# Moving a weight matrix to the end of the load stream: where the product of w2 is loaded and summed

## The chip, the cores and the metric

One core of one Trainium2 chip. The metric is the device time of one execution in microseconds. PE is the matmul engine and PSUM the memory that it adds its results up in; DMA is the loading from memory. The profile records for PE a granted clock, a share of full speed: 1.0 is called warm here, 0.5 cold. In the first measurement the kernel before took 194.74 to 194.83 us in four runs. Later batches ran on other chips, each beside its own runs of the kernel before (medians 194.63, 194.84, 195.00 for a single run, and 194.69), so experiments are compared with the kernel before of their own batch. Its single runs scattered more in those batches than in the first: from 194.44 to 195.08 over eleven runs, from 194.56 to 195.22 over eleven, from 194.60 to 195.05 over eight.

## The reference, cut to what matters

Attention for one new token in two batch rows, over the last 4096 positions of 8 key/value heads, plus a dense layer on the same normalised input, plus the input:

```python
def reference(A_x, A_k_cache, A_v_cache, A_wq, A_wo, B_x, B_w1, B_b1, B_w2):
    xn = _layernorm(A_x, axis=-1)                    # 2 rows of 448
    return A_x + attention(xn, k_cache, v_cache, wq) @ wo + mish(xn @ w1 + b1) @ w2
# w2: 1792 x 448, bf16. Keys and values used: 16 (head, row) pairs, 2 MB of keys and 2 MB of values each.
```

Nearly all of it is loading: 77.7 MB for 3810 instructions of work. Everything is summed in two PSUM banks, `psA[0]` and `psA[1]`, of 2 x 224 values each: the input, the w2 product and the wo product.

## The kernel before

The parts that matter (cuts marked with `...`):

```python
def add(n, lhsT, rhs, **flags):                 # every psA matmul: 2 weight columns, 224 moving
    nc.tensor.matmul(psA[n][:, :], lhsT=lhsT, rhs=rhs, skip_group_check=True, **flags)

def load_dense():                               # near the start: w1, then w2 whole
    dense["w1"] = ...
    dense["w2"] = v_tile(NX * NF * D)...
    nc.sync.dma_start(out=dense["w2"], in_=B_w2.rearrange("(x q c) d -> q x c d", x=NX, q=P))

def dense_out():                                # 28 psA matmuls, at step 1 of 18
    for x in range(NX):
        for c in range(NF):
            for n in range(NO):
                add(n, act_bf[:, c, x, :], w2_sb[:, x, c, n * DO : (n + 1) * DO], ...)

def values(i):                                  # 64 matmuls: 128 weight columns, 2 moving
    ...
def mix(kvh):                                   # 8 psA matmuls with wo rows
    ...

for i in range(NK + KA):                        # NK = 16 heads x rows, KA = 2
    if i + 2 < NK: load_k(i + 2)
    if i < NK:
        load_v(i, parts=1 if i < NK - 1 else 2)         # the last values in two transfers
        if b == Bsz - 1:
            load_wo(kvh, parts=1 if i < NK - 1 else 2)
        ...                                             # scores of head i
    if i == 1: dense_out()
    if i >= KA:
        values(i - KA)
        if b == Bsz - 1: mix(kvh)
# then copy psA[0], psA[1] to SBUF and store
```

All large loads are issued in this order by one engine, SyncE, and in the traces here PE's matmuls follow one another in the order of the program. So at the end PE has, in a fixed line: values of the last head, then its wo product.

The softmax here doesn't subtract the row's maximum and nothing guards it: scores larger than these inputs give would overflow.

## Time and profile before

| what | value | from |
|---|---|---|
| median time | 194.76 us | four runs |
| span of the profiled execution | 192.7 us | the page |
| share of DMA in the chain that ended last | 96% | the page |
| last landing of values | 187.21 us | the chain in order of time |
| PE done | 190.19 us | the chain in order of time |
| w2 product, in the middle | 28 matmuls in 2.84 us | PE's timeline |

The lines themselves, and how these times follow from one another, stand in the prediction.

### The profile page before, as it was taken

What the parts mean: (1) busy time and instruction counts of PE and PEld (TensorE: products, weight loads), DVE (VectorE), ACT (ScalarE), POOL (GpSimd) and SP (SyncE); (2) the same over time, 40 slices, a digit from 0 to 9 for tenths busy, and PEclk for the clock granted to TensorE, in tenths of its full rate; (3) what the DMA queues carried; (4) which work ended last, traced back from release to release, by engine and by line L of the source; (5) the groups of instructions that cost most, each with busy time, mean ns of one, the idle gap of its engine ahead of it and who ended that gap; (6) DMA issues with size and microseconds to landing.
All of it is one profiled execution on the core that took longest, in us unless ns stands there. A gap on an engine that the chain in (4) does not pass through costs nothing.

```text
span 192.7 us, 3810 instructions
## 1 busy us (share of the span) xinstructions
PE 130.4 (68%) x1624; PEld 81.3 (42%) x1624; DVE 102.2 (53%) x137; ACT 25.5 (13%) x69; POOL 24.8 (13%) x138
## 2 busy tenths in 40 slices
PE   0242993999827985499709881797449592898854
PEld 0142381466513654246504651364324452364752
DVE  4605506996638390929264753838091744748101
ACT  5000110112200211012200220021101110021100
POOL 7004320022110112002200210020200200000000
PEclk9999996699995799669975998599957979589965
DMA  6999999999999999999999999999999999999960
GB/s 211 424 447 408 427 427 435 428 435 402 431 422 428 425 415 428 435 418 414 429 425 432 420 416 430 428 425 411 428 432 428 403 434 422 432 414 429 410 253 2
DMA packets 7674, 77.90 MB, mean 404 GB/s; under 512 B 741, under 2 KB 2793, under 8 KB 3050
## 3 DMA queue, kind: packets, MB, share of 16 engines
q1 hardware_dynamic: 7652, 77.66, 96.1%
q8 instruction: 12, 0.20, 0.4%
q14 instruction: 4, 0.03, 0.0%
q10 hardware_dynamic: 6, 0.01, 0.0%
HBM read 77.67 MB, written 0.00 MB: 403 GB/s over the span
## 4 chain that ended last, share of the span: by engine, by line
DMA 96%; PE 1%; SPq 1%; issue 0%; ACT 0%; DVE 0%
DMA v<-in_A_v_cache_dram 51%; DMA k<-in_A_k_cache_dram 18%; DMA wo<-in_A_wo_dram 17%; DMA v<-in_B_w_dram 10%; PE psA L201 1%; PE o L411 1%; SPq L109 0%; SPq L325 0%; ACT res L484 0%; DVE oT L422 0%; SPq L336 0%
## 5 line engine op out<-in xcount | busy, mean ns | idle before, releaser
L352 DVE STREAM_TRANSPOSE kt<-k 128x2048 f32<-128x2048 f32 x32 | 73.5, 2300 | 48.9 <-DMA k<-in_A_k_cache_dram 48.9
L364 PE MATMUL sc<-kt,qdiag 128*128 128x512 bf16 x256 | 75.0, 443 | 14.4 <-DVE kt L352 14.3
L364 PEld LDWEIGHTS <-qdiag 128*128 128x128 bf16 x256 | 26.1, 111 | 50.5 <-issue 24.1
L374 ACT ACTIVATE p<-sc 128x512 bf16<-128x512 f32 x32 | 19.1, 597 | 144.8 <-PE sc L364 140.9
L244 POOL COPY qdiag<-qrep 32x8 bf16<-32x8 bf16 x128 | 21.0, 186 | 125.3 <-PE sc L364 109.8
L201 PE MATMUL psA<-wo,oT 128*2 128x224 bf16 x64 | 12.5, 370 | 31.3 <-DVE oT L422 31.3
L411 PEld LDWEIGHTS <-v 128*128 128x128 bf16 x1024 | 27.9, 97 | 6.3 <-DMA v<-in_A_v_cache_dram 3.0
L411 PE MATMUL o<-pT,v 128*128 128x2 bf16 x1024 | 28.1, 163 | 2.7 <-DMA v<-in_A_v_cache_dram 2.7
L385 DVE STREAM_TRANSPOSE pT<-p 128x512 bf16<-128x512 bf16 x32 | 21.4, 671 | 0.0
L201 PEld LDWEIGHTS <-oT 128*2 128x2 bf16 x64 | 6.5, 111 | 34.6 <-DVE oT L422 32.0
L393 PEld LDWEIGHTS den<-hsel,rs 128*128 128x128 f32 x64 | 11.7, 227 | 3.8 <-issue 2.1
L401 DVE RECIPROCAL rec<-den 128x2 f32<-128x2 f32 x16 | 2.5, 153 | 18.7 <-PE den L393 18.7
L393 PE MATMUL den<-hsel,rs 128*128 128x2 f32 x64 | 9.4, 252 | 0.0
L215 PE MATMUL qT_ps<-xs,v 128*128 128x4 bf16 x112 | 3.3, 166 | 6.1 <-DMA v<-in_A_wq_dram 6.1
L422 DVE TENSOR_TENSOR oT<-o,rec 128x4 bf16<-128x4 f32 x16 | 2.1, 134 | 8.5 <-PE o L411 8.5
L374 ACT ACTIVATION_READ_ACCUMULATOR p<-sc 128x1 f32 x32 | 6.2, 194 | 0.0
L215 PEld LDWEIGHTS <-v 128*128 128x128 bf16 x112 | 3.1, 104 | 6.6 <-DMA v<-in_A_wq_dram 6.6
L224 DVE CAST qT<-qT_ps 128x64 bf16<-128x64 f32 x1 | 0.2, 225 | 7.0 <-PE qT_ps L215 7.0
L169 PE MATMUL xnT_ps<-ident,xn_bf 2*128 2x2 bf16 x7 | 0.5, 166 | 5.0 <-DVE xn_bf L133 5.0
L270 PE MATMUL hT_ps<-xs,v 128*128 128x4 bf16 x49 | 3.7, 195 | 0.0
L270 PEld LDWEIGHTS <-v 128*128 128x128 bf16 x49 | 3.2, 149 | 0.3
L201 PE MATMUL psA<-v,act_bf 128*2 128x224 bf16 x28 | 2.8, 259 | 0.0
(40 smaller groups left out, 22.5 us busy)
## 6 DMA issues: line engine op xcount, KB each, us to landing
k<-in_A_k_cache_dram SPq DMA_DIRECT2D x16, 2048.0 KB, 32.5
v<-in_A_v_cache_dram SPq DMA_DIRECT2D x15, 2048.0 KB, 34.8
v<-in_B_w_dram SPq DMA_DIRECT2D x2, 1568.0 KB, 21.2
wo<-in_A_wo_dram SPq DMA_DIRECT2D x7, 448.0 KB, 31.8
v<-in_A_wq_dram SPq DMA_DIRECT2D x1, 2048.0 KB, 7.8
v<-in_A_v_cache_dram SPq DMA_DIRECT2D x2, 1024.0 KB, 29.9
v<-in_A_wq_dram SPq DMA_DIRECT2D x1, 1536.0 KB, 11.1
wo<-in_A_wo_dram SPq DMA_DIRECT2D x2, 224.0 KB, 24.1
```

The source lines that it names most:

```text
L201: nc.tensor.matmul(psA[n][:, :], lhsT=lhsT, rhs=rhs, skip_group_check=True, **flags)
L215: nc.tensor.matmul(qT_ps[:, hh, e, :], lhsT=wq_v[s][:, hh, e, :], rhs=xs[:, s, :, :].rearrange("p x b -> p (x b)"), start=(s == 0), stop=( ...
L244: nc.gpsimd.tensor_copy(out=tv[rows, :, e, j * Q : j * Q + rep], in_=qrep[rows, :, h0 : h0 + rep, e, x, b],)
L270: nc.tensor.matmul(hT_ps[:, c, :, :].rearrange("p x b -> p (x b)"), lhsT=w1_v[:, s, c, :], rhs=xs[:, s, :, :].rearrange("p x b -> p (x b)" ...
L352: nc.vector.transpose(out=kt[:].bitcast(FP32), in_=k[:, half * TH * Dh : (half + 1) * TH * Dh].bitcast(FP32),)
L364: nc.tensor.matmul(psc[:], lhsT=qdiag[i % NW][:, n * NE + e, :], rhs=ktv[:, n, e, :, :], start=(n == 0 and e == 0), stop=(n == NB - 1 and ...
L374: nc.scalar.activation(out=p_sb[:], in_=psc[:].rearrange("p t c -> p (t c)"), func=ACT.Exp, scale=scale, accum_out=state["rs", i][:, s % N ...
L385: nc.vector.transpose(out=pT[:], in_=p_t.pop(s)[:])
L393: nc.tensor.matmul(den[:], lhsT=rs[:, n : n + 1].to_broadcast([P, P]), rhs=hsel[:], start=(n == 0), stop=(n == NH - 1),)
L401: nc.vector.reciprocal(out=state["rec", i][:], in_=den[:])
L411: nc.tensor.matmul(po[:, c, :], lhsT=vv[:, t, c, :], rhs=pTv[:, th, 0:rep], start=(t == 0 and c == 0), stop=(t == T - 1), skip_group_check ...
L422: nc.vector.tensor_tensor(out=oT[:, :, :, b], in0=po[:], in1=state.pop(("rec", i))[:].unsqueeze(1).to_broadcast([P, ND, rep]), op=ALU.mult,)
```

## The change

The intent: after the last bytes land there should be as little work as possible. So w2, which needs nothing but the dense activations that have long been ready, is loaded last, in three parts (14, 10 and 4 matmuls' worth, into a buffer that held keys before), and its product closes the sum. Only the third part (4 matmuls) is then behind the last landing. In exchange the last values and the last wo rows are each one transfer again.

```diff
-        dense["w2"] = v_tile(NX * NF * D).rearrange(...)
-        nc.sync.dma_start(out=dense["w2"], in_=B_w2.rearrange(...))
+    W2 = ((0, 0, NF), (1, 0, NF - 2), (1, NF - 2, NF))
+    def load_w2():
+        t = k_pool.tile([P, T * Dh], BF16, tag="k", name="k")
+        ...
+        for x, lo, hi in W2:
+            nc.sync.dma_start(out=t[:, x, lo:hi, :], in_=w2_in[:, x, lo:hi, :])
...
-            load_v(i, parts=1 if i < NK - 1 else 2)
+            load_v(i)
...
-                load_wo(kvh, parts=1 if i < NK - 1 else 2)
+                load_wo(kvh)
+            if i == NK - 1:
+                load_w2()
...
-        if i == 1:
-            dense_out()
         if i >= KA:
             values(i - KA)
             ...
+    dense_out()
```

`dense_out` now runs by part, bank and chunk, and its last matmul on each bank closes the group.

More of the change, by code (lines that the diff above doesn't have):

```diff
@@ L251, with load_w1 @@
     dense = {}
-    def load_dense():
+    def load_w1():
         dense["w1"] = v_tile(NS * HF).rearrange("p (s n) -> p s n", s=NS)
@@ L258, in load_dense @@
         )
-        dense["w2"] = v_tile(NX * NF * D).rearrange("p (x c d) -> p x c d", x=NX, c=NF)
-        nc.sync.dma_start(
-            out=dense["w2"], in_=B_w2.rearrange("(x q c) d -> q x c d", x=NX, q=P)
-        )
+    W2 = ((0, 0, NF), (1, 0, NF - 2), (1, NF - 2, NF))
+    def load_w2():
+        t = k_pool.tile([P, T * Dh], BF16, tag="k", name="k")
+        t = t[:, 0 : NX * NF * D].rearrange("p (x c d) -> p x c d", x=NX, c=NF)
+        w2_in = B_w2.rearrange("(x q c) d -> q x c d", x=NX, q=P)
+        for x, lo, hi in W2:
+            nc.sync.dma_start(out=t[:, x, lo:hi, :], in_=w2_in[:, x, lo:hi, :])
+        dense["w2"] = t
     def dense_in():
@@ L305, in dense_out @@
         w2_sb = dense.pop("w2")
-        for x in range(NX):
-            for c in range(NF):
-                for n in range(NO):
+        for x, lo, hi in W2:
+            for n in range(NO):
+                for c in range(lo, hi):
                     add(
@@ L313, in dense_out @@
                         start=False,
-                        stop=False,
+                        stop=(x == NX - 1 and c == NF - 1),
                     )
@@ L328, in load_k, with load_v, load_wo @@
         k_t[i] = t
-    def load_v(i, parts=1):
+    def load_v(i):
         kvh, b = heads[i]
-        t = v_tile(T * Dh).rearrange("p (t d) -> p t d", t=T)
-        vin = A_v_cache[b, kvh, s0:Sk, :].rearrange("(p t) d -> p t d", p=P)
-        for u in range(parts):
-            ts = slice(u * T // parts, (u + 1) * T // parts)
-            nc.sync.dma_start(out=t[:, ts, :], in_=vin[:, ts, :])
-        v_t[i] = t
-    def load_wo(kvh, parts=1):
+        t = v_tile(T * Dh)
+        nc.sync.dma_start(
+            out=t, in_=A_v_cache[b, kvh, s0:Sk, :].rearrange("(p t) d -> p (t d)", p=P)
+        )
+        v_t[i] = t.rearrange("p (t d) -> p t d", t=T)
+    def load_wo(kvh):
         w = wo_pool.tile([P, rep, ND * D], BF16, tag="wo", name="wo")
@@ L342, in load_wo @@
         win = A_wo[r0 : r0 + rep * Dh, :].rearrange("(h p c) d -> p h (c d)", h=rep, p=P)
-        for u in range(parts):
-            hs = slice(u * rep // parts, (u + 1) * rep // parts)
-            nc.sync.dma_start(out=w[:, hs, :], in_=win[:, hs, :])
+        nc.sync.dma_start(out=w[:], in_=win)
         wo_t[kvh] = w
@@ L439, in mix @@
                         start=False,
-                        stop=(kvh == Hkv - 1 and h == rep - 1 and c == ND - 1),
+                        stop=False,
                     )
@@ L446 @@
     load_k(0)
-    load_dense()
+    load_w1()
     load_k(1)
```

## The prediction

> **What bounds the kernel now.** I read the page first (busy shares, the slices, the chain that ended last), then the chain in order of time, then PE's timeline and the windows of the last 13 us.
>
> ```profile
> PE   0242993999827985499709881797449592898854
> PEclk9999996699995799669975998599957979589965
> DMA  6999999999999999999999999999999999999960
> GB/s 211 424 447 408 427 427 435 428 435 402 431 422 428 425 415 428 435 418 414 429 425 432 420 416 430 428 425 411 428 432 428 403 434 422 432 414 429 410 253 2
> DMA 96%; PE 1%; SPq 1%; issue 0%; ACT 0%; DVE 0%
> ```
>
> From the second slice to slice 38 the DMA engines are 90% busy or more and move 402 to 447 GB/s; 96% of the final chain is DMA. The kernel is one stream of 77.7 MB. PE, 68% busy, has room in the middle. So the time is: start, the stream, and what is left to do after the last bytes. The end of the chain in order of time:
>
> ```profile
> 156.59 30.62 DMA v<-in_A_v_cache_dram
> 187.21 0.05 issue
> 187.26 1.02 PE o L411 x32
> 188.28 0.02 issue
> 188.31 0.18 DVE oT L422
> 188.48 0.04 issue
> 188.53 1.67 PE psA L201 x8
> 190.19 0.02 issue
> 190.22 0.34 ACT res L484
> ```
>
> The second half of the last values lands at 187.21; 32 value matmuls, the normalisation and 8 wo matmuls follow, PE is done at 190.19: a tail of 2.98 us. The last 2.5 us (190.2 to 192.7) are the copy and the output's way home, the same in both kernels. The second wo half is issued at 166.38 and takes 21.9 us (the smallest time to landing of wo), so the stream itself ends at 188.3, in the shadow of the value matmuls.
>
> PE's timeline and the windows at the end:
>
> ```profile
> 180.32 0.93 PE L201 MATMUL psA<-wo,oT 128*2 128x224 bf16 x8 [0.26 <-DVE oT L422]
> ...
> 182.29 1.75 PE L411 MATMUL o<-pT,v 128*128 128x2 bf16 x64 [0.50 <-DMA v<-in_A_v_cache_dram]
> 184.78 1.01 PE L411 MATMUL o<-pT,v 128*128 128x2 bf16 x32 [0.73 <-DMA v<-in_A_v_cache_dram]
> 187.26 1.01 PE L411 MATMUL o<-pT,v 128*128 128x2 bf16 x32 [1.47 <-DMA v<-in_A_v_cache_dram]
> 188.53 1.65 PE L201 MATMUL psA<-wo,oT 128*2 128x224 bf16 x8 [0.26 <-DVE oT L422]
> ```
>
> ```profile
> 182.00:184.00 2.00, 1.71 (x64) 1.67 (x64) 0.00 (x0) 0.00 (x0) 0.00 (x0) 1.00 1.01 422
> 184.00:186.00 2.00, 1.06 (x34) 0.93 (x32) 0.17 (x1) 0.00 (x0) 0.00 (x0) 0.53 0.85 331
> 186.00:188.00 2.00, 0.74 (x28) 0.75 (x29) 0.00 (x0) 0.00 (x0) 0.00 (x0) 0.50 0.25 91
> 188.00:190.20 2.20, 1.92 (x19) 1.02 (x15) 0.52 (x2) 0.00 (x0) 0.00 (x0) 0.50 0.00 0
> ```
>
> In these rows the columns after PE, PEld, DVE, ACT, POOL are the granted clock, the DMA share and GB/s. The same eight 224-column matmuls take 0.93 us at clock 1.0 and 1.65 us at clock 0.5. The clock fell at about 184.1 though PE had just run 64 value matmuls[...]. DMA falls from 0.85 to 0.25 before the last landing[...].
>
> [...] cold at 184.1, and elsewhere the full clock came back at 64.6, 5.4 us after dense work had begun at 59.22. [...] (1.65 and 0.93 us less one latency of 0.39 and 0.26, over 7: 180 and 96 ns; 180 includes a shorter first step). [...]
>
> **The change part by part.** w2 is 1792 x 448 x 2 B = 1.606 MB. The rate at the end, from the last two value halves, is 1.049 MB in 187.26 - 184.78 = 2.48 us, 423 GB/s.
>
> *Bytes.* None is added or removed. All traffic before the last wo rows now lands earlier by 1.606 MB / 423 GB/s = 3.80 us, w2 comes after, the stream ends again at about 188.3.
>
> *Landings, counted back from 188.3.* The third part of w2 (229 KB) at 188.3, the second (573 KB) at 187.8, the first (803 KB) at 186.4, wo at 184.5, the last values, now whole, at 187.21 - 3.80 = 183.4.
>
> *Removed.* The 28 w2 matmuls in the middle (2.84 us at clock 1.0, 39.15 to 41.99) leave a stretch in which PE is not the bound: no gain. Gone from the end: the wait for the second value half and the tail after it.
>
> *Added at the end on PE, in program order.* 64 value matmuls begin at 183.4 + 0.05 and take 1.75 us (27 ns each at either clock: 32 took 1.01 cold, 64 took 1.75 warm): 185.2. Normalisation and start of the next burst, as from 188.28 to 188.53, 0.25: 185.45. Then 8 wo matmuls and 28 for w2 on the same two banks, 36 in a row. Cold, 36 x 0.187 + 0.2 for the last one's latency = 6.9 us: 192.4. Warm, 36 x 0.096 + 0.2 = 3.7: 189.1.
>
> *Which clock.* Everything before is earlier by 3.8, so the last score burst (before: done at 178.3) is done at 174.5; then come 128 value matmuls, 8 for wo, and an idle stretch from about 180.2 to 183.4. That is less work than what lost the clock before, so the burst starts cold. [...] Back at 188.0: 14 done, 22 x 0.096 + 0.2 = 2.3, end 190.3. Back at 191.4: 32 done, end 192.0. Mean about 191.1. [...] it ends at 192.4; I give that 30%.
>
> *Sum.* 0.7 x 191.1 + 0.3 x 192.4 = 191.5, against 190.19 before: +1.3 us. The last w2 landing (188.3 plus 4 matmuls, 0.8 us: 189.1) is **not** the last wait in this account: w2's first part is there at 186.4, while PE gets to it at 185.45 + 8 x 0.187 = 186.9. The change turns a tail bound by a landing into one bound by a cold PE.
>
> **The rivals.**
>
> *1. The intended gain.* PE keeps up, and only four matmuls follow the last landing: 189.1, 1.1 us less than before, 193.7. For it: after the last bytes there is much less to do than 72 matmuls' worth of waiting in two halves. Against: 36 matmuls in 188.3 - 185.45 = 2.9 us need 80 ns each, under even the warm 96. At full clock the two limits meet; it needs a warm PE at 185.4. About 10%.
>
> *2. The stream itself changes.* Without w2 early, a value buffer is free sooner, and transfers might be issued sooner. But the stream is never short of work: the transfers wait 30 us from issue to landing and DMA is 90% busy throughout, so hidden: 0. A stall because w2 waits for a key buffer: the keys of head 12 were turned long before, also 0. [...]
>
> *3. Landing of the last values later than 183.4*[...]. Every 0.1 us there is 0.1 us at the end, as PE is in line behind it.
>
> **Range and chances.** Rounding the sum down a little for the chance of rival 1: 194.77 + 1.15 = 195.9. The low end, 194.4, is warm soon with a stream slightly faster; the high end, 197.3, is a burst cold throughout (+2.2) with a little more. 2% is 3.9 us, more than any of these: within 2% 0.96, faster 0.01, slower 0.03.
>
> **What would show it right or wrong.** The last values land at about 183.4 and the 64 value matmuls start there without a second wait. The last 36 psA matmuls run without a gap of any DMA from about 185.4, with granted clock 0.5 at first and 187 ns apart, and PE ends 1 us or so later than 190.19. The final chain should then hold about 6 us of PE in place of 2.7, and its last DMA should be the values, not w2. Times of single runs should scatter more than the 0.09 us of before[...]. It is wrong if the last wait of PE is for w2 (rival 1: the clock then is 1.0 in the burst), if the last values land much from 183.4, or if the stream ends elsewhere than at 188.3.

The sum: 0.7 x 191.1 + 0.3 x 192.4 = 191.5 against 190.19, so +1.3 us, rounded down to 1.15. Its terms: the clock should come back between 188.0 and 191.4 (of which 191.1 is the mean end), and a burst cold to the end (192.4) should have 30%. Read both as guesses, and "less work than what lost the clock before" as an estimate from one fall, that at 184.11 in the kernel before. The spacings in it are measured in the kernel before: in the burst from 188.53, at clock 0.5, matmuls start 187 ns apart; at 180.32, at clock 1.0, eight of them take 0.93 us, less one of 0.26 and over 7, 96 ns.

## The result, and the profile after

The changed kernel took 194.94, 195.39, 195.69 and 195.82 us: median 195.54, against 194.76. The ratio is 1.0035, 95% interval 1.0011 to 1.0060. (A ratio here is the mean time of one kernel's fast runs over that of the other's of the same rounds, so not quite the ratio of the medians.) So it is slower by about 0.7 us, well within 2%; and its runs scatter over 0.88 us where those of the kernel before scatter over 0.09 in this batch (over 0.45 to 0.66 in the later ones).

The page's rate of transfer and its chain, for the kernel after:

```profile
GB/s 221 426 440 416 439 434 424 421 424 414 431 424 434 417 421 424 434 415 420 431 428 428 421 416 424 428 417 428 424 428 406 445 424 424 416 425 424 399 215 2
DMA 94%; PE 4%; SPq 0%; issue 0%; ACT 0%; DVE 0%
```

The stream is what it was: no slice of the middle falls under 406 GB/s (402 before). In the chain DMA's share went from 96 to 94%, PE's from 1 to 4%. The end of the chain in order of time (start, length, what):

```profile
151.81 31.74 DMA v<-in_A_v_cache_dram
183.55 0.05 issue
183.60 1.88 PE o L414 x64
185.48 0.02 issue
185.50 0.17 DVE oT L425
185.68 0.04 issue
185.72 4.92 PE psA L201 x36
190.64 0.02 issue
190.66 0.33 ACT res L488
```

The last DMA in the chain is the values, not w2. From 183.60 on PE works 6.8 us with no wait but the normalisation. The windows of the same stretch (after PE, PEld, DVE, ACT and POOL: granted clock, DMA share, GB/s):

```profile
182.00:184.00 2.00, 0.40 (x15) 0.41 (x16) 0.00 (x0) 0.00 (x0) 0.00 (x0) 0.50 1.03 404
184.00:186.00 2.00, 1.74 (x58) 1.59 (x55) 0.16 (x1) 0.00 (x0) 0.00 (x0) 0.50 0.76 305
186.00:188.00 2.00, 2.00 (x13) 1.34 (x11) 0.00 (x0) 0.00 (x0) 0.00 (x0) 0.50 0.28 111
188.00:190.00 2.00, 2.00 (x21) 1.66 (x20) 0.00 (x0) 0.00 (x0) 0.00 (x0) 0.90 0.00 0
```

From 186 to 188 PE is fully busy and gets through 13 matmuls at clock 0.5; from 188 to 190, at 0.90 on average, through 21. DMA has nothing left to move after 188: the last of the three w2 transfers is issued at 167.6 and takes 20.8 us, so it is there at about 188.4, 2.2 us before PE is done. PE is behind the data, at half clock.

### The profile page after: what moved, and what is told of

Its sections match the earlier page's. It is cut to its first block, busy times and chain, and to the rows that moved or that the text cites. A ratio compares the mean times of both kernels' runs of the same rounds, so it can differ in the third digit from the quotient of the medians.

```text
span 193.2 us, 3810 instructions
## 1 busy us (share of the span) xinstructions
PE 134.6 (70%) x1624; PEld 83.4 (43%) x1624; DVE 102.3 (53%) x137; ACT 25.4 (13%) x69; POOL 24.8 (13%) x138
## 4 chain that ended last, share of the span: by engine, by line
DMA 94%; PE 4%; SPq 0%; issue 0%; ACT 0%; DVE 0%
DMA v<-in_A_v_cache_dram 35%; DMA k<-in_A_k_cache_dram 35%; DMA wo<-in_A_wo_dram 18%; DMA v<-in_A_wq_dram 5%; PE psA L201 3%; PE o L414 1%; SPq L109 0%; ACT res L488 0%; DVE oT L425 0%; SPq L339 0%; SPq L331 0%
## 5 line engine op out<-in xcount | busy, mean ns | idle before, releaser
L367 PE MATMUL sc<-kt,qdiag 128*128 128x512 bf16 x256 | 78.4, 459 | 12.7 <-DVE kt L355 12.0
L367 PEld LDWEIGHTS <-qdiag 128*128 128x128 bf16 x256 | 27.2, 115 | 50.8 <-issue 28.7
L396 PEld LDWEIGHTS den<-hsel,rs 128*128 128x128 f32 x64 | 13.1, 255 | 4.3 <-issue 2.5
L396 PE MATMUL den<-hsel,rs 128*128 128x2 f32 x64 | 10.6, 270 | 0.0
L201 PE MATMUL psA<-k,act_bf 128*2 128x224 bf16 x28 | 3.5, 290 | 0.0
## 6 DMA issues: line engine op xcount, KB each, us to landing
k<-in_B_w_dram SPq DMA_DIRECT2D x1, 560.0 KB, 25.2
```

Of the source, the lines that this page charges most:

```text
L367: nc.tensor.matmul(psc[:], lhsT=qdiag[i % NW][:, n * NE + e, :], rhs=ktv[:, n, e, :, :], start=(n == 0 and e == 0), stop=(n == NB - 1 and ...
L396: nc.tensor.matmul(den[:], lhsT=rs[:, n : n + 1].to_broadcast([P, P]), rhs=hsel[:], start=(n == 0), stop=(n == NH - 1),)
```

## The experiments

The theory, called A in the expectations: PE's line of work after the last values sets the end, and its clock sets how long that line is. Its rival, B: the landing of w2 sets the end. All outputs are right.

The trace keeps a record of PE's granted clock: it is 1.0 or 0.5. Near the end it rises at 170.46 and falls at 184.11 in the profile of the kernel before; in the changed kernel's it rises at 174.76, falls at 181.59 and rises again at 188.41. For the experiments it is read from its mean over stretches of 1 or 2 us. What sets the times of these switches is not shown here.

### The changed kernel again (after_again, after_third)

No edit.

> The changed kernel itself, once more, as the yardstick of this chip. Theory A (the end is set by PE's line of 64 value and 36 psA matmuls at a halved clock, and by when the clock comes back): median 195.3 to 195.8, single runs scattered over 0.5 us or more, granted clock 0.5 at the start of the 36. Theory B (the end is set by the landing of w2's third part): the same median, but scatter like that of the kernel before, 0.1 us, and a DMA as the last wait of PE.

> One more look at the changed kernel[...]. Theory A: the burst of 36 begins at clock 0.5 again; the later in it the clock comes back (0.5 to 1.0), the later the end, by about half of the delay.

Measured: median 195.29, runs from 194.96 to 196.57, ratio to the kernel before 1.0043 (1.0021 to 1.0064). The single look took 195.17. The median of the first was a hair under the range expected of it, the scatter is there, and in both profiles the burst starts cold, at 185.66 and 185.79. The full clock comes back at about 188.3 in the first profile (mean clock 0.50 from 186 to 188, 0.92 from 188 to 190), at about 188.8 in the second (0.50, then 0.80); PE is done at 190.56 and 190.87. The later return goes with the later end. The profiles did not catch the slowest run (196.57), so what that one did is not seen. Its span on the core is 194.1 us, against 193.1 to 193.8 of the other five: so about half a microsecond of its excess lies outside the span, and PE's work lies within it.

### A warm PE (e1_warm) and the same instructions without columns (e2_narrow)

The kernel holds eight PSUM tiles, one of which is free after the start. Fillers are written there:

```diff
+    def keep_busy(n, cols):
+        for _ in range(n):
+            nc.tensor.matmul(state["spare"][:, 0:cols], lhsT=ident[:, :],
+                rhs=qdiag[0][:].rearrange("p n c -> p (n c)")[:, 0:cols],
+                start=True, stop=True, skip_group_check=True)
...
+        if i == NK:
+            state["spare"] = ps_m.tile([P, 512], FP32, tag="m", name="spare")
+            keep_busy(4, 512)          # e2_narrow: 2 columns in place of 512
+        if i == NK + 1:
+            keep_busy(9, 512)          # e2_narrow: 2 columns in place of 512
         if i >= KA:
             values(i - KA)
```

> The changed kernel with 13 matmuls of 512 columns into a bank that nobody reads, 4 ahead of the values of the last head but one and 9 ahead of the last values, where PE waits for a DMA anyway. Theory A: the clock is 1.0 when the 36 psA matmuls begin, they run 96 ns apart, PE ends near 189.3 instead of 190.6 to 191.5, so 193.6 to 194.0, less than the kernel before; and the scatter shrinks to 0.1 or 0.2 us. Theory B: no gain, 195.5.

> As e1_warm, with the same 13 matmuls of 2 columns each: the instructions without the streamed columns. Theory A: they do not hold the clock, so as the changed kernel, 195.3 to 195.8, with its scatter. If instead the mere presence of instructions on PE (or a changed issue) made e1_warm faster, this one is faster too, near 194.

Measured: e1_warm took 193.73, 194.04, 194.81, 195.28, 195.33 and 195.52, ratio 1.0008 (0.9982 to 1.0035). The expected speed was reached by two runs of six, and the scatter did not shrink: a half miss. e2_narrow took 194.99 to 196.35, ratio 1.0064 (1.0043 to 1.0084), like the changed kernel or a little worse; the two intervals overlap. So 13 more instructions of 2 columns gained nothing, and 13 of 512 columns did in two runs of six. In the profiles the clock from 182 to 188 was 0.50 with the narrow fillers and 1.00 with the wide ones. These two kernels do not separate columns from busy time, for the narrow fillers also took only 0.60 us together. Two stretches of the traces show that busy time alone does not tell: in e2_narrow PE was busy 3.18 us of the 4.00 from 178 to 182, mostly with matmuls of 2 columns, and the clock was lost at about 181.6 (mean 0.90 from 180 to 182, then 0.50); in the changed kernel's profile of the first batch it was busy only 1.82 of the 3.50 from 147.50 to 151.00, most of it with score matmuls of 512 columns, and the clock stayed at 1.0, until 157.69. What does tell is not shown. The profile of e1_warm is of one of its fast runs (194.04), PE's timeline:

```profile
183.64 1.75 PE L414 MATMUL o<-pT,v 128*128 128x2 bf16 x64 [0.17 <-DMA v<-in_A_v_cache_dram]
185.65 0.93 PE L201 MATMUL psA<-wo,oT 128*2 128x224 bf16 x8 [0.26 <-DVE oT L425]
186.84 2.89 PE L201 MATMUL psA<-k,act_bf 128*2 128x224 bf16 x28 [0.26 <-DMA k<-in_B_w_dram]
```

The values start at the same time as in the changed kernel (183.64), the 8 wo matmuls take 0.93 us in place of 1.65, and now PE is ahead of the data: it waits 0.26 us for w2. PE is done at 189.74. That is the mechanism of A, seen in one run; what spoils the slow runs is taken up below.

### The last values in halves again (e3_halves)

```diff
-            load_v(i)
+            load_v(i, parts=1 if i < NK - 1 else 2)      # load_v as in the kernel before
```

> The changed kernel with the last values in two transfers again, as the kernel before has them. Theory A: the first 32 value matmuls run before 183.55 and the psA burst begins 0.85 us sooner, near 184.85, still cold; [...] the end comes 0.4 to 0.9 us sooner: 194.6 to 195.1. Theory B: the landing of w2 is unmoved, 195.5.

Measured: median 194.99 (194.84 to 195.54), ratio 1.0025 (1.0012 to 1.0038), so about 0.3 us under the changed kernel of the same batch (194.99 against 195.29). In the profile, of one of the slower runs (195.54), the psA burst starts at 184.94, 0.72 us before that of the changed kernel's profile, but the clock comes back only at about 190.0 (mean 0.50 from 188 to 190, 0.98 from 190 to 191), and the w2 product, from 186.71, takes 4.46 us. The median lies in the expected range, but an earlier start at half speed is worth less than it looks. The two medians differ by less than either kernel's own scatter, and the intervals of their ratios (1.0012 to 1.0038, 1.0021 to 1.0064) overlap: that undoing this part gives time back is likely, and not shown.

### w2 in one transfer (e4_one_part)

```diff
-        for x, lo, hi in W2:
-            nc.sync.dma_start(out=t[:, x, lo:hi, :], in_=w2_in[:, x, lo:hi, :])
+        nc.sync.dma_start(out=t, in_=w2_in)
```

> The changed kernel with w2 as one transfer. Its landing, near 188.5, then holds all 28 of its products, with PE's clock cold after a gap. Theory A: the 28 begin at 188.5 in place of 187.2, at 187 ns each until the clock comes back, PE ends between 192.5 and 193.9: 197.2 to 198.5, 2 us or more over the changed kernel. Theory B (only the last landing counts): within 0.5 us of the changed kernel, as that landing is unmoved.

Measured: median 198.05, ratio 1.0164 (1.0141 to 1.0187). PE's timeline:

```profile
185.82 1.65 PE L201 MATMUL psA<-wo,oT 128*2 128x224 bf16 x8 [0.26 <-DVE oT L424]
188.97 4.18 PE L201 MATMUL psA<-k,act_bf 128*2 128x224 bf16 x28 [1.50 <-DMA k<-in_B_w_dram]
```

All 28 wait for the whole of w2, at 188.9, and then run mostly cold: the clock is 0.50 from 188 to 190 and 0.56 on average from 190 to 192. The three parts are worth some 2.5 us within this change (198.05 against 195.17 to 195.54; by the ratios, 1.0164 against 1.0035 and 1.0043). A kernel whose last landing is 0.5 us later (188.9 against 188.4) and which is 2.5 us slower speaks against B: the work behind the landing counts, not the landing alone.

### Fillers spread out (e7_spread), a fourth part (e8_spread_4), and why runs fall in two groups (e7_look2, e7_look3)

e7_spread has the same 13 fillers, placed so:

```diff
 # keep_busy and the spare bank as in e1_warm, the bank taken at i == NK - 1
 # in values(i), in the loop over t
+            if t == TH and i in (NK - 3, NK - 2):
+                keep_busy(3 if i == NK - 3 else 2, 512)
 # in the main loop
+        if i == NK:
+            keep_busy(2, 512)
+        if i == NK + 1:
+            keep_busy(6, 512)
```

e8_spread_4 adds one more cut of w2:

```diff
-    W2 = ((0, 0, NF), (1, 0, NF - 2), (1, NF - 2, NF))
+    W2 = ((0, 0, 4), (0, 4, NF), (1, 0, NF - 2), (1, NF - 2, NF))
```

> As e1_warm, whose fast runs took 193.7 to 194.0 and whose slow ones 194.8 to 195.5, with the same 13 matmuls of 512 columns spread: 3 inside the values of head 13, 2 ahead of and 2 inside those of head 14, 6 ahead of the last. Theory A, with my reading of the slow runs of e1_warm (the clock was lost before its dummies began, so they ran at half speed and came late): fewer slow runs, median 193.8 to 194.4. If the scatter of e1_warm has another cause: median about 195 as there.

> e7_spread with w2's first part cut once more (4 and 3 chunks), as in e1_warm's profile the warm PE waited for that part until 186.8. Theory A: 0.3 to 0.5 us under e7_spread, 193.4 to 194.0, PE's last wait then being for w2. Theory B: likewise near the floor of the stream, 193.4 to 193.8. This is the candidate to beat both kernels.

Measured: e7_spread 193.71, 193.83, 193.85 and 195.20, 195.41, 195.72: two groups, median 194.52, ratio 0.9989 (0.9956 to 1.0022). e8_spread_4 193.84 to 195.56, ratio 0.9992. Both expectations missed. The fourth part gained nothing even in fast runs: in its profile PE no longer waits for w2's first part, but then waits for the part with the first five chunks of the second half, landed at 188.00, and has 14 matmuls to do from there on (10 of that part, 4 of the last):

```profile
188.04 1.50 PE L201 MATMUL psA<-k,act_bf 128*2 128x224 bf16 x14 [0.24 <-DMA k<-in_B_w_dram]
```

For the two groups, two more looks at the same kernel:

> A second look at e7_spread, whose runs fell in two groups (193.7 to 193.9 and 195.2 to 195.7). Theory A with cold fillers: if this run is of the slow group, its profile shows clock 0.5 in some filler matmuls (427 ns apart), the last values begun 0.5 us or more after they landed, and the psA burst later; if it is of the fast group, clock 1.0 throughout as in the first look. Rival (the stream of that run was slower): in a slow run the values land later and the fillers run at clock 1.0.

> A third look at e7_spread, the same two readings: of the slow group with half-speed fillers and late values (theory A), or late landings at clock 1.0 (rival), or of the fast group and then telling nothing new.

(The 427 ns are those of the 512-column score matmuls at clock 0.5 in the kernel before, which start 426 or 427 ns apart from 166.63 on; at clock 1.0, from 173.82 on, 216 to 219.) Both looks were of the slow group (195.26 and 195.17), and neither expectation held. PE's timeline of the first:

```profile
181.22 1.46 PE L450 MATMUL spare<-qdiag,ident 128*128 128x512 bf16 x6
183.69 1.75 PE L416 MATMUL o<-pT,v 128*128 128x2 bf16 x64 [1.02 <-DMA v<-in_A_v_cache_dram]
185.70 1.65 PE L201 MATMUL psA<-wo,oT 128*2 128x224 bf16 x8 [0.26 <-DVE oT L427]
187.15 3.81 PE L201 MATMUL psA<-k,act_bf 128*2 128x224 bf16 x28
```

The six fillers take 1.46 us, at clock 1.00 (from 180 to 184), and the values land at their usual time: neither slow fillers nor a slow stream. But the fillers are done at 182.68, and then come 1.0 us of waiting and 1.75 us of value matmuls that stream 2 columns each. The clock is lost at about 185.7, just as the burst begins (mean 1.00 from 182 to 184, 0.93 from 184 to 186, then 0.50). The second look is alike: 0.97 us of waiting, 0.89 from 184 to 186, then 0.50. The fast look, e7_spread's own profile, has

```profile
182.02 1.46 PE L450 MATMUL spare<-qdiag,ident 128*128 128x512 bf16 x6
```

In that run the last scores ended about 0.8 us later (the values behind them begin at 175.59 in place of 174.78), so the same fillers ran until 183.48, the last values followed at 183.50 without a wait, and the clock was 1.00 from 184 to 190. In these three profiles fast thus goes with fillers that reach up to the values, slow with a gap of 1.0 us before them. That the gap loses the clock is my estimate from these three; e10_fill tests it. My reading of e1_warm's slow runs had the sign wrong for these: the fillers ended too early, not too late.

### Fillers up to the landing (e10_fill)

```diff
+            if t == TH and i in (NK - 3, NK - 2):
+                keep_busy(2, 512)
...
+        if i == NK:
+            keep_busy(2, 512)
+        if i == NK + 1:
+            keep_busy(9, 512)
         if i >= KA:
             values(i - KA)
+            if i == NK + 1:
+                keep_busy(1, 512)
```

> The slow looks at e7_spread had their fillers at full speed but done 1 us before the last values landed; [...] the clock was lost just at the burst. Here 16 fillers: 2 inside the values of head 13, 2 ahead of and 2 inside those of head 14, 9 ahead of the last values, 1 after them. Theory A: [...] few or no runs above 195.0, median 193.8 to 194.4[...]. Rival (the two groups do not come from the clock): two groups as in e7_spread, median about 194.5 to 195.

Measured: 193.75, 193.78, 193.78, 193.86 and 193.88; ratio 0.9952 (0.9938 to 0.9966). PE's timeline:

```profile
181.81 2.10 PE L450 MATMUL spare<-qdiag,ident 128*128 128x512 bf16 x9
183.75 1.74 PE L416 MATMUL o<-pT,v 128*128 128x2 bf16 x64
185.75 0.93 PE L201 MATMUL psA<-wo,oT 128*2 128x224 bf16 x8 [0.26 <-DVE oT L427]
186.55 2.89 PE L201 MATMUL psA<-k,act_bf 128*2 128x224 bf16 x28
```

With nothing taken from PE and 16 useless matmuls added, the kernel is 1.6 to 1.8 us faster than the changed one (other chips, so by the ratios to the kernels before of their own batches: 0.9952 against 1.0035 and 1.0043), 0.9 us faster than the kernel before, and the scatter is gone: 0.13 us, where the kernel before has 0.45 in this batch. Its profile has clock 1.00 in every stretch from 182 to 190. Its runs have mean clocks of 0.839 to 0.858, so the clock was not the same in all of them; the one profile is like that of e7_spread's fast look (the values of the last head but one begin at 175.60, there at 175.59, in the slow looks at 174.78 and 174.76). For the changed kernel this settles A: same bytes, the last values there by 183.75 (against 183.49 to 183.63), same product; PE's clock differs. With PE warm the landing of w2 comes into play again: in the profiles of e1_warm, e7_spread and e8_spread_4 the last DMA of the chain is a part of w2.

### The kernel before with a smaller last piece of values (e11_small_last)

The conclusion, turned on the kernel before: put less PE work behind the last landing, and leave w2 early.

```diff
-        for u in range(parts):
-            ts = slice(u * T // parts, (u + 1) * T // parts)
-            nc.sync.dma_start(out=t[:, ts, :], in_=vin[:, ts, :])
+        cuts = (0, T) if parts == 1 else (0, TH, T - 4, T)     # T = 32, TH = 16
+        for lo, hi in zip(cuts, cuts[1:]):
+            nc.sync.dma_start(out=t[:, lo:hi, :], in_=vin[:, lo:hi, :])
```

> The kernel before (w2 early) with the last values cut in 16, 12 and 4 of their 32 steps in place of 16 and 16, so that only 8 of the 64 value matmuls wait for the last landing. From its profile: 187.21 + 0.05 + 0.3 for the 8 + 0.25 = 187.85 for the wo burst, whose second half waits for the last wo rows at 188.33; PE ends at 189.4 to 189.7 in place of 190.19. Theory A (what counts is PE's work behind the last landings, at a cold clock): 0.4 to 0.7 us under the kernel before, 194.1 to 194.4, with its small scatter. Rival (the end is the stream's own): no gain.

Measured: median 194.12 (194.07 to 194.21), ratio 0.9969 (0.9955 to 0.9983), as expected. PE's timeline:

```profile
186.70 1.01 PE L411 MATMUL o<-pT,v 128*128 128x2 bf16 x32 [0.87 <-DMA v<-in_A_v_cache_dram]
188.07 1.65 PE L201 MATMUL psA<-wo,oT 128*2 128x224 bf16 x8 [0.35 <-DMA wo<-in_A_wo_dram]
```

The last 8 value matmuls no longer wait by themselves; the last wait is now for wo rows, and PE is done at 189.73 (expected: 189.4 to 189.7), at clock 0.5. It takes no filler and has little scatter.

## Why the prediction was right

**The stream is unmoved: right.** The last w2 part was put at 188.3; it landed at about 188.4. **The last values land at 183.4: nearly right**, 183.55.

**PE's line: right in kind, a little too short.** I had 64 value matmuls in 1.75 us and the burst from 185.45; they took 1.87 us and it began at 185.72. I had said that these 64 take the same time at either clock. They do not quite: 1.87 us at half clock, 1.74 in e10_fill's warm run.

**The fall of the clock: seen, its cause not shown.** The prediction has the clock cold at 184.1 in the kernel before. The trace shows that, though PE was busy 1.71 of the 2.00 us from 182 to 184, at clock 1.00, with 64 matmuls that stream 2 columns each; the clock fell at 184.11. The spacings that the prediction reckons with are measured in the changed kernel's burst as well: 187 ns before the clock came back, 96 after.

**A cold start and a clock that comes back within the burst: right.** The estimate for the return was 188.0 to 191.4. In the changed kernel's three profiles it came at 188.41, about 188.3 and about 188.8, at the early end; but the profiles caught two of the fastest runs and one middling one. PE was done at 190.64, 190.56 and 190.87, against an estimated 190.3 to 192.0. Every timed run's span is on record, and in the profiles 2.5 us of it follow PE's end. From the spans of the ten timed runs (193.1 to 194.1, mean 193.5) I therefore estimate ends of 190.6 to 191.6, mean 191.0: the 191.1 of the prediction for a clock that comes back.

**The size of the sum: too large.** Predicted were 1.15 us more; the two batches gave ratios of 1.0035 and 1.0043, which of 194.77 is 0.7 to 0.8 us. The term that was mis-sized is the burst cold to its end, to which I gave 30% and an end at 192.4. It was not seen: in all three profiles the clock came back within the burst, 2.7, 2.7 and 3.0 us after its start, and from that start on PE ran nothing but matmuls of 2 weight and 224 moving columns. That term had added 0.3 x 1.3 = 0.4 us to the expected end, the whole excess or nearly so.

**The range: no test of the mechanism.** 194.4 to 197.3 held a burst that is soon warm and one that is cold throughout. That the time fell inside says little; the landings, the cold start and the point of return say more.

**Scatter: right, though its measure was lucky.** Foretold was more than 0.09 us; it was 0.88 and 1.61 us (some half a microsecond of the latter outside the span), and 0.13 us once PE was held at full clock. But the 0.09 of the kernel before was a quiet batch: 0.64, 0.66 and 0.45 followed.

**Rival 1: rightly not chosen, and its floor was mis-sized.** I said that a warm PE would end at 189.1, with four matmuls after the last landing. With a warm PE (e7_spread's fast look, e10_fill) it ended at 189.45. In e10_fill it waited for no part of w2: its burst began at 185.75 in place of 185.45, which is most of the difference. An earlier start would have gained little, for the second part lands at about 187.9 (issued at 162.7, 25.2 us), with 10 + 4 matmuls of 96 ns and one latency behind it: 187.9 + 1.3 + 0.2 = 189.4. In e8_spread_4 PE did wait for that part, landed at 188.00, and ended at 189.55. I had followed only the last part.

The shortest account of it all, an estimate from these figures: one psA matmul uses 128 x 224 x 2 B = 57 KB of w2. At 423 GB/s the stream delivers that in 136 ns. A warm PE needs 96 ns for it (the spacing within the burst in e10_fill) and keeps ahead; a cold one needs 187 ns (the changed kernel's, before the clock came back) and falls behind with every matmul. So at half clock each chunk of w2 moved behind the values makes the end later, and at full clock sooner. The change was right for a PE that it did not have.

What stays open: what the slowest runs of e1_warm and of the changed kernel (196.57) looked like inside, as no profile caught one; whether e10_fill also holds the clock in runs whose last scores end as early as in e7_spread's slow looks, of which its five fast runs are the only sign; and what exactly holds or loses the clock. No run here could choose when the clock switches.

## What to carry to other kernels

At the end of a load-bound kernel, compare for each piece the time in which it lands with the time in which the engine works it off, at the clock which that engine will have there; put last what is worked off faster than it lands. Do not take the matmul duration from the busy middle: here PE, after waiting for the stream, ran at half speed (187 ns a matmul in place of 96), and then moving work behind the last bytes cost time. If the move needs the full clock, check that it is held up to the very start of the burst, in several runs, as the times at which the clock switches differ from run to run (back at 188.41, about 188.3 and about 188.8 in three profiles of the changed kernel).
